# Taking engine orders from a scheduler with a re-tuned priority list, in an attention plus channel-mix kernel

## Chip, cores, metric

One core of one Trainium2 chip. The metric is device microseconds of one execution; lower is better. A kernel's time is the median of its runs. The spans in the traces are about 1.7 us shorter than the times (297.6 against 299.3 us for the profiled execution of the kernel before), because they run from the first to the last instruction.

## The reference

Batch 8, 8 heads, 576 positions, head dimension 64. Four heads attend to the last 32 positions, four to every fourth of the last 128. The attention output, laid out as x with 512 channels, goes through a channel mix:

```python
scores = where(mask, q @ k.T / 8, -1e9);  x = softmax(scores) @ v      # 8 batches
x_prev = x shifted by one position
xk = mu_k*x + (1-mu_k)*x_prev;   xr = mu_r*x + (1-mu_r)*x_prev
k  = relu(xk @ w_k);             v = (k*k) @ w_v                       # 512->1024->512
out = sigmoid(xr @ w_r) * v
```

## The kernel before

The kernel cuts the work into small steps and issues them from a list sorted by position. For attention, one batch needs T (transposes of q and k), six S (scores on TensorE, exp on ScalarE, mask multiply on VectorE), six P (value matmul on TensorE; reciprocal and multiply on VectorE) and three X (transposes of x; copies on ScalarE). S and P work on one block each, a stretch of 96 positions, so a batch has six blocks. A block also needs the 32 rows of v before it, its halo rows, which an on-chip shuffle copies into place. Then comes the interpolation, here called lerp: dx, md, xk, and md, xr on VectorE (dx is x minus x_prev; md is dx times murep, which holds mu - 1 repeated along the positions). The channel mix has nine tiles of 512 rows, each with eight K groups, four R groups and eight V groups of four matmuls.

```python
    def step_lerp_d(b):                        # dx: three VectorE operations
        ...
    def step_lerp_m(b, w):                     # md = dx * murep
        ...
    def plan_attn(b, base, cad, t0, tcad):
        ...
        for i in range(NB):
            at(base + cad * i, lambda i=i: step_S(b, i))
            at(base + cad * i + 2.2, lambda i=i: step_P(b, i))
            if i % 2 == 1:
                at(base + cad * i + 3.8, lambda i=i: step_X(b, i // 2))
        end = base + cad * 5 + 3.8
        at(end + 0.2, lambda: step_lerp_d(b))
        at(end + 0.3, lambda: step_lerp_m(b, 0))
        at(end + 0.4, lambda: step_lerp_a(b, 0))
        ...
    # ... (cut)
    with tc.manual_schedule(engines={ET.PE, ET.Activation, ET.DVE, ET.Pool}):
        for n in range(6):
            step_T(0, n, "act" if n % 2 == 0 else "dve")
        fix_v(0)                               # on-chip shuffle of v's halo rows
        make_murep(0); make_murep(1)           # 8 ScalarE copies
        ...
        for _, _, f in sorted(order, key=lambda t: t[:2]):
            f()
```

`manual_schedule` means that the named engines execute the program in the order in which it is written. Engines not named get an order from the compiler's scheduler, which takes the order of writing as a priority only. The order is fixed at compile time either way. In the traces an engine then waits at the next instruction in its order: in the run "The scheduler alone" below, VectorE stood 3.00 us at a scaling of wv, although the dx for the md behind it had been done for longer than that.

The softmax here doesn't subtract the row's maximum and nothing guards it: scores larger than these inputs give would overflow.

## Time and profile before

| | before |
|---|---|
| time, median (range), 3 runs | 298.81 us (297.08 to 299.91) |
| span of the profiled run | 297.6 us |
| ramp, to the first K matmul of tile 0 | 41.1 us |
| seven stages (tile 0 to 6, with attention of batches 1 to 7) | 217.2 us |
| tail (tiles 7 and 8, no attention left) | 39.3 us |

Two lines of the page. The first gives busy time, share of the span and instruction count of each engine; the second gives the clock that TensorE was granted in 40 equal slices of the span, in tenths of full speed.

```profile
PE 239.5 (80%) x2448; PEld 123.1 (41%) x2448; DVE 179.6 (60%) x349; ACT 158.5 (53%) x281; POOL 76.3 (26%) x123
...
PEclk9999999998699968999899979997999799999999
```

TensorE is the busiest engine, at 80%, and its clock dips in several slices (mean 0.954). The next view cuts the span at the first K matmul of each tile. Its columns are: the stretch, its length, busy us of TensorE, its weight loads, VectorE, ScalarE and GpSimd with instruction counts, granted clock, share of the DMA engines, GB/s. The first row is the ramp, then come stages 0 to 6.

```profile
0.00:41.09 41.09, 13.56 (x216) 10.67 (x217) 21.46 (x77) 16.30 (x26) 28.98 (x54) 1.00 1.67 147
41.09:75.18 34.09, 28.68 (x328) 14.39 (x328) 21.72 (x44) 19.80 (x35) 14.71 (x22) 0.96 1.46 153
75.18:107.47 32.29, 28.91 (x345) 15.45 (x345) 19.97 (x35) 20.67 (x37) 9.69 (x14) 0.92 0.66 86
107.47:143.26 35.79, 31.09 (x337) 15.69 (x338) 23.42 (x41) 19.93 (x36) 9.39 (x14) 0.88 0.72 96
143.26:174.30 31.04, 27.06 (x298) 13.63 (x297) 20.56 (x36) 18.21 (x33) 8.13 (x12) 0.94 0.70 96
174.30:205.08 30.78, 27.00 (x299) 13.70 (x298) 20.49 (x36) 18.21 (x33) 5.36 (x8) 0.94 0.56 90
205.08:235.80 30.72, 26.94 (x298) 13.63 (x298) 20.43 (x36) 18.22 (x33) 0.00 (x0) 0.94 0.13 35
235.80:258.28 22.48, 21.61 (x177) 10.36 (x177) 15.96 (x30) 13.09 (x24) 0.00 (x0) 0.99 0.13 36
```

Stages 3 to 5 (rows 143.26 to 235.80) take 30.7 to 31.0 us each with TensorE busy 27 us at a clock of 0.94. Who waits for whom on TensorE in the stages (us in total, times, longest; the 13.1 us include 5.3 us at the end of the ramp):

```profile
PE xo L236 <- DVE AT L221: 15.3, 4, 4.0
PE mm L310 <- DVE xk L298: 13.1, 4, 5.3
```

One such wait, in order of time. First VectorE, then TensorE; columns are start, duration, engine, line, operation, output and inputs, shapes, count, and in brackets the idle time before it and who ended it.

```profile
165.91 1.06 DVE L278 TENSOR_TENSOR dx<-xT 128x1728 f16<-128x1728 f16 x1 [2.63 <-ACT xT L268]
...
169.06 1.43 DVE L298 TENSOR_TENSOR xk<-md,xT 128x1024 f16<-128x1024 f16 x2
170.40 0.68 DVE L337 SCALAR_TENSOR_TENSOR ot<-sg,mm 128x512 f32<-128x512 f32 x1
171.00 0.55 DVE L221 TENSOR_TENSOR AT<-AT,mk 128x768 f16<-128x768 f16 x1
```

```profile
171.60 0.40 PE L236 MATMUL xo<-VAp,AT 128*128 128x65 f16 x4 [3.98 <-DVE AT L221]
171.82 0.41 PE L236 MATMUL xo<-VAd,AT 128*128 128x65 f16 x4
172.04 1.90 PE L333 MATMUL mm<-wv,k 128*128 128x512 f16 x4
```

VectorE does dx, md and xk of one batch in one row (165.91 to 170.4) and an output multiply (`ot`), and only then the mask multiply (`AT`) of the next batch, whose exp had ended at 166.65. TensorE stands idle 3.98 us for that mask multiply (`AT` in brackets). Its next four V matmuls take 1.90 us; the four before the hole took 1.03. After the hole the clock is half (0.50 from 171.6 to 174.8 by windows).

In the ramp, the chain of work that ended last reads (start, us, what):

```profile
14.28 5.31 ACT murep L127 x8
19.59 0.70 ACT AT L218
```

The eight murep copies sit in front of the first exp in ScalarE's queue.

### The profile page before, as it was taken

To read this page: it belongs to the slowest core of one execution; us is meant where nothing else is said; L and a number is where in the kernel's file an instruction comes from. 1 tells how busy PE (TensorE), PEld (TensorE's weight loads), DVE (VectorE), ACT (ScalarE), POOL (GpSimd) and SP (SyncE) were. 2 spreads that over 40 slices of the span, in tenths; PEclk is the share of its full clock that TensorE was granted. 3 is DMA by queue.
4 is the path that set the end of the run, shared out by engine and by line. 5 is a ranking of instruction groups with operands and counts; after the bars stand their busy time and mean duration, and the time that the engine had idled before them with its cause. 6 is when DMAs were issued, how large, how long until landed. Compare 5 with 4: busy or idle time off the path is not lost.

```text
span 297.6 us, 6026 instructions
## 1 busy us (share of the span) xinstructions
PE 239.5 (80%) x2448; PEld 123.1 (41%) x2448; DVE 179.6 (60%) x349; ACT 158.5 (53%) x281; POOL 76.3 (26%) x123
## 2 busy tenths in 40 slices
PE   0625349994889969994999599968998699899993
PEld 0513215442445634552455245533553344444441
DVE  4266392587377576558765676568656877772321
ACT  1484308853585737753586448643874285352530
POOL 8586575407210550037001800060000000000000
PEclk9999999998699968999899979997999799999999
DMA  8999999999391697039901990192011201113222
GB/s 87 146 166 198 134 169 172 138 127 162 44 154 39 96 134 138 0 82 122 200 3 37 137 202 29 37 126 79 2 37 37 70 3 37 35 72 87 56 63 78
DMA packets 57403, 27.80 MB, mean 93 GB/s; under 512 B 31776, under 2 KB 51744, under 8 KB 57376
## 3 DMA queue, kind: packets, MB, share of 16 engines
q0 software_dynamic: 49920, 16.78, 61.4%
q1 hardware_dynamic: 7456, 10.64, 11.9%
q8 instruction: 19, 0.31, 0.5%
q14 instruction: 8, 0.07, 0.1%
HBM read 33.56 MB, written 9.44 MB: 144 GB/s over the span
## 4 chain that ended last, share of the span: by engine, by line
PE 62%; DVE 19%; ACT 11%; issue 3%; DMA 3%; POOL 0%; POOLq 0%; DVEq 0%
PE mm L310 22%; PE mm L333 16%; PE mm L322 7%; PE xo L236 4%; DVE md L285 4%; DVE x L242 3%; PE tb L185 3%; PE ps L215 3%; PE tb L189 3%; ACT AT L218 3%; DVE dx L278 3%; DMA qk<-in_k_dram 3%; DVE xk L298 2%; DVE AT L221 2%; ACT murep L127 2%
## 5 line engine op out<-in xcount | busy, mean ns | idle before, releaser
L310 PE MATMUL mm<-xk,wk 128*128 128x512 f16 x288 | 77.5, 408 | 13.1 <-DVE xk L298 13.1
L333 PE MATMUL mm<-wv,k 128*128 128x512 f16 x288 | 75.8, 393 | 0.0
L315 ACT ACTIVATE kr<-mm 128x512 f16<-128x512 f32 x72 | 43.1, 601 | 38.1 <-PE mm L310 36.4
L218 ACT ACTIVATE AT<-ps 128x768 f16<-128x768 f32 x48 | 38.9, 810 | 34.2 <-PE ps L215 34.2
L77 POOL DMA_DIRECT2D VAp<-in_v_dram x32 | 23.1, 727 | 93.8 <-PE xo L236 92.4
L310 PEld LDWEIGHTS <-wk 128*128 128x128 f16 x288 | 26.2, 103 | 43.0 <-issue 15.5
L317 DVE TENSOR_TENSOR k<-kr 128x1024 f16<-128x1024 f16 x36 | 24.8, 691 | 31.7 <-ACT kr L315 31.7
L221 DVE TENSOR_TENSOR AT<-AT,mk 128x768 f16<-128x768 f16 x48 | 26.7, 557 | 25.1 <-ACT AT L218 25.0
L337 DVE SCALAR_TENSOR_TENSOR ot<-sg,mm 128x512 f32<-128x512 f32 x36 | 24.6, 684 | 23.7 <-PE mm L333 21.8
L322 PE MATMUL mm<-wr,xr 128*128 128x512 f16 x144 | 37.0, 379 | 0.0
L325 ACT ACTIVATE sg<-mm 128x512 f32<-128x512 f32 x36 | 21.6, 600 | 28.7 <-PE mm L322 28.6
L333 PEld LDWEIGHTS <-k 128*128 128x128 f16 x288 | 25.9, 100 | 26.5 <-issue 2.2
L242 DVE TENSOR_TENSOR x<-xo,rec 96x512 f16<-96x512 f32 x48 | 33.0, 687 | 1.6
L236 PE MATMUL xo<-VAp,AT 128*128 128x65 f16 x192 | 15.0, 204 | 21.7 <-DVE AT L221 15.3
L236 PEld LDWEIGHTS <-AT 128*128 128x128 f16 x384 | 18.0, 104 | 33.6 <-DVE AT L221 18.3
L168 ACT ACTIVATE QKp<-tb 128x384 f16<-128x384 f16 (+1 forms) x31 | 19.1, 645 | 11.1 <-PE tb L185 11.0
L168 ACT ACTIVATE QKd<-tb 128x768 f16<-128x768 f16 (+1 forms) x29 | 18.4, 659 | 8.7 <-PE tb L189 8.7
L85 POOL DMA_DIRECT2D VAd<-in_v_dram x32 | 19.9, 630 | 11.1 <-DMA qk<-in_k_dram 5.8
L185 PE MATMUL tb<-ident,qk 48*64 48x48 f16 (+1 forms) x512 | 15.1, 207 | 9.3 <-DMA qk<-in_q_dram 7.2
L285 DVE TENSOR_TENSOR md<-dx,murep 128x2304 f16<-128x2304 f16 x16 | 21.7, 1355 | 0.3
L215 PE MATMUL ps<-QKp 64*128 64x96 f16 x192 | 13.5, 221 | 7.1 <-ACT AT L218 7.0
L185 PEld LDWEIGHTS <-qk 48*64 48x64 f16 (+1 forms) x512 | 12.1, 117 | 16.7 <-DMA qk<-in_q_dram 7.2
(50 smaller groups left out, 245.6 us busy)
## 6 DMA issues: line engine op xcount, KB each, us to landing
qk<-in_q_dram POOLq DMA_DIRECT2D x8, 384.0 KB, 6.3
qk<-in_k_dram POOLq DMA_DIRECT2D x8, 384.0 KB, 8.5
VAp<-in_v_dram POOLq DMA_DIRECT2D x32, 72.0 KB, 4.8
out_dram<-ot SPq DMA_DIRECT2D x8, 256.0 KB, 2.5
out_dram<-ot SPq DMA_DIRECT2D x8, 224.0 KB, 2.5
qk<-in_q_dram POOLq DMA_DIRECT2D x8, 192.0 KB, 9.3
qk<-in_k_dram POOLq DMA_DIRECT2D x8, 192.0 KB, 9.1
VAd<-in_v_dram POOLq DMA_DIRECT2D x16, 96.0 KB, 4.3
```

The costliest lines, as they stand in the source:

```text
L168: nc.scalar.activation(out=out, in_=in_, func=AF.Copy)
L185: nc.tensor.transpose(out=tv[par * D:(par + 1) * D, wi, sl, :], in_=t[:nj, w, 2 * hp + par, r * D:(r + 1) * D], identity=ident[:nj, :nj])
L218: nc.scalar.activation(out=at[:, :, :, 0:QB], in_=ps[:, :, 0:4 * QB].rearrange("p a (s x) -> p a s x", s=4), func=AF.Exp, scale=0.125)
L221: nc.vector.tensor_tensor(out=at[:, :, :, 0:QB], in0=at[:, :, :, 0:QB], in1=MK[combos[i]], op=ALU.mult)
L236: nc.tensor.matmul(out=xo[:, pr, par * (D + 1):(par + 1) * (D + 1)], lhsT=w, rhs=va[:, o + par:o + par + D + 1], start=True, stop=True)
L242: nc.vector.tensor_tensor(out=x16[:QB].rearrange("p a g d -> p g a d"), in0=xo[:QB, :, 1:VW].rearrange("p g (a d) -> p g a d", a=2), in1=r ...
L285: nc.vector.tensor_tensor(out=md, in0=xT_of[(b, "dx")], in1=murep[:, w], op=ALU.mult)
L310: nc.tensor.matmul(out=pk, lhsT=wk[:, c, f * 128:(f + 1) * 128], rhs=xk_t[tt][:, c], start=(c == 0), stop=(c == 3))
L315: nc.scalar.activation(out=kr[:, f % 2], in_=pk, func=AF.Relu, scale=8.0)
L317: nc.vector.tensor_tensor(out=k2_of[tt][:, f - 1:f + 1], in0=kr, in1=kr, op=ALU.mult)
L322: nc.tensor.matmul(out=pr, lhsT=xr_t[tt][:, c, ts * 128:(ts + 1) * 128], rhs=wr[:, c], start=(c == 0), stop=(c == 3))
L333: nc.tensor.matmul(out=pv, lhsT=k2_of[tt][:, f, ts * 128:(ts + 1) * 128], rhs=wv[:, f], start=(f == 0), stop=(f == 7))
```

## The change

Its intent is to let the scheduler order TensorE, ScalarE and VectorE, with a list tuned for that: attention starts earlier against the tiles, the value step lags more, the interpolation is issued in six pieces. In the ramp, murep goes from ScalarE to VectorE, the masks need 8 copies in place of 32, the mask construction on GpSimd goes ahead of the loads of v, and the transposes of x come one step later. The core of the diff:

```diff
-    load_batch(0)
+    for jc in range(2):
+        load_qk(0, jc)                  # load_v(0) now follows the mask work
...
-            nc.scalar.activation(out=murep[:, w, c], in_=ones, func=AF.Copy, scale=mu[:, w, c:c + 1])
+            nc.vector.tensor_scalar(out=murep[:, w, c], in0=ones, scalar1=mu[:, w, c:c + 1], scalar2=None, op0=ALU.mult)
...
-    def plan_attn(b, base, cad, t0, tcad):
+    def plan_attn(b, base, cad, t0, tcad, lag=2.2):
...
-            at(base + cad * i + 2.2, lambda i=i: step_P(b, i))
+            at(base + cad * i + lag, lambda i=i: step_P(b, i))
...
-        at(end + 0.2, lambda: step_lerp_d(b))
-        at(end + 0.3, lambda: step_lerp_m(b, 0))
-        at(end + 0.4, lambda: step_lerp_a(b, 0))
-        at(end + 2.5, lambda: step_lerp_m(b, 1))
-        at(end + 4.5, lambda: step_lerp_a(b, 1))
+        at(end + 0.2, lambda: step_lerp_d(b, 0))
+        at(end + 0.8, lambda: step_lerp_d(b, 1))
+        at(end + 1.3, lambda: step_lerp_m(b, 0))
+        at(end + 2.0, lambda: step_lerp_a(b, 0))
+        at(max(end + 4.0, G * b + 2.5), lambda: step_lerp_m(b, 1))
+        at(max(end + 5.5, G * b + 4.5), lambda: step_lerp_a(b, 1))
...
-    plan_attn(1, 8.0, 1.5, 4.2, 0.7)    # likewise for batches 2 and 3
+    plan_attn(1, 6.3, 1.4, 3.0, 0.6)
-        base = G * (b - 1) - 3.5
-        plan_attn(b, base, 3.0, base - 16.5, 3.0)
+        base = G * (b - 1) - 6
+        plan_attn(b, base, 3.0, base - 16.5, 3.0, 3.0)
...
-    with tc.manual_schedule(engines={ET.PE, ET.Activation, ET.DVE, ET.Pool}):
+    with tc.manual_schedule(engines={ET.Pool}):
```

More of the change, by code (lines that the diff above doesn't have):

```diff
@@ L123 @@
     murep = const.tile([128, 2, 4, S], FP16, name="murep")
-    def make_murep(w):
+    for w in range(2):
         for c in range(4):
-            nc.scalar.activation(out=murep[:, w, c], in_=ones, func=AF.Copy, scale=mu[:, w, c:c + 1])
+            nc.vector.tensor_scalar(out=murep[:, w, c], in0=ones, scalar1=mu[:, w, c:c + 1], scalar2=None, op0=ALU.mult)
     m01 = const.tile([128, 3, QB], FP16, name="m01")
@@ L142, with make_masks @@
     MK = {}
-    for combo in ((START, START), (FULL, START), (FULL, MID), (FULL, FULL)):
-        t = const.tile([128, 2, 4, QB], FP16, name=f"mk{combo[0]}{combo[1]}")
-        for par in range(2):
-            for sl in range(4):
-                nc.vector.tensor_copy(out=t[:, par, sl], in_=m01[:, combo[sl // 2]])
-        MK[combo] = t
+    def make_masks(combos):
+        for combo in combos:
+            t = const.tile([128, 2, 4, QB], FP16, name=f"mk{combo[0]}{combo[1]}")
+            for g in range(2):
+                nc.vector.tensor_copy(out=t[:, :, 2 * g:2 * g + 2],
+                                      in_=m01[:, combo[g]].unsqueeze(1).unsqueeze(1).to_broadcast([128, 2, 2, QB]))
+            MK[combo] = t
+    load_v(0)
     combos = [(START, START), (FULL, START), (FULL, MID), (FULL, MID), (FULL, FULL), (FULL, FULL)]
@@ L273, with step_lerp_d @@
     xk_t, xr_t = {}, {}
-    def step_lerp_d(b):
+    def step_lerp_d(b, part):
         xT = xT_of[b]
-        dx = lerp_p.tile([128, 4, S], FP16, name="dx")
-        nc.vector.tensor_tensor(out=dx[:, :, J:S], in0=xT[:, :, J:S], in1=xT[:, :, 0:S - J], op=ALU.subtract)
-        nc.vector.tensor_tensor(out=dx[:, :, 1:J], in0=xT[:, :, 1:J], in1=xT[:, :, 3 * J:S - 1], op=ALU.subtract)
-        nc.vector.tensor_copy(out=dx[:, :, 0:1], in_=xT[:, :, 0:1])
-        xT_of[(b, "dx")] = dx
+        if part == 0:
+            xT_of[(b, "dx")] = lerp_p.tile([128, 4, S], FP16, name="dx")
+        dx = xT_of[(b, "dx")]
+        if part == 0:
+            nc.vector.tensor_tensor(out=dx[:, :, J:S], in0=xT[:, :, J:S], in1=xT[:, :, 0:S - J], op=ALU.subtract)
+        else:
+            nc.vector.tensor_tensor(out=dx[:, :, 1:J], in0=xT[:, :, 1:J], in1=xT[:, :, 3 * J:S - 1], op=ALU.subtract)
+            nc.vector.tensor_copy(out=dx[:, :, 0:1], in_=xT[:, :, 0:1])
     def step_lerp_m(b, w):
@@ L365, in plan_attn @@
             at(t0 + tcad * 5 + 0.1, lambda: [load_qk(b + 2, jc) for jc in range(2)])
-            at(base + cad * 5 + 2.3, lambda: load_v(b + 2))
+            at(base + cad * 5 + lag + 0.1, lambda: load_v(b + 2))
         at(base - 2, lambda: fix_v(b))
@@ L369, in plan_attn @@
             at(base + cad * i, lambda i=i: step_S(b, i))
-            at(base + cad * i + 2.2, lambda i=i: step_P(b, i))
+            at(base + cad * i + lag, lambda i=i: step_P(b, i))
             if i % 2 == 1:
-                at(base + cad * i + 3.8, lambda i=i: step_X(b, i // 2))
-        end = base + cad * 5 + 3.8
-        at(end + 0.2, lambda: step_lerp_d(b))
-        at(end + 0.3, lambda: step_lerp_m(b, 0))
-        at(end + 0.4, lambda: step_lerp_a(b, 0))
-        at(end + 2.5, lambda: step_lerp_m(b, 1))
-        at(end + 4.5, lambda: step_lerp_a(b, 1))
+                at(base + cad * i + lag + 2.4, lambda i=i: step_X(b, i // 2))
+        end = base + cad * 5 + lag + 2.4
+        at(end + 0.2, lambda: step_lerp_d(b, 0))
[4 more added lines that the diff above has]
+        at(max(end + 5.5, G * b + 4.5), lambda: step_lerp_a(b, 1))
     G = 20
@@ L389 @@
     at(-2, lambda: load_batch(2))
-    plan_attn(1, 8.0, 1.5, 4.2, 0.7)
-    plan_attn(2, 25.0, 1.7, 18.5, 1.0)
-    plan_attn(3, 41.5, 2.0, 33.5, 1.3)
+    plan_attn(1, 6.3, 1.4, 3.0, 0.6)
+    plan_attn(2, 24.5, 1.7, 18.5, 0.9)
+    plan_attn(3, 41.0, 2.0, 33.5, 1.3)
     for b in range(4, B):
-        base = G * (b - 1) - 3.5
-        plan_attn(b, base, 3.0, base - 16.5, 3.0)
-    with tc.manual_schedule(engines={ET.PE, ET.Activation, ET.DVE, ET.Pool}):
+        base = G * (b - 1) - 6
+        plan_attn(b, base, 3.0, base - 16.5, 3.0, 3.0)
+    with tc.manual_schedule(engines={ET.Pool}):
         for n in range(6):
             step_T(0, n, "act" if n % 2 == 0 else "dve")
+        make_masks([(START, START)])
         fix_v(0)
-        make_murep(0)
-        make_murep(1)
         step_S(0, 0)
         for i in range(NB):
+            if i == 0:
+                make_masks([(FULL, START)])
             if i + 1 < NB:
                 step_S(0, i + 1)
+            if i == 0:
+                make_masks([(FULL, MID), (FULL, FULL)])
+            if i in (2, 4):
+                step_X(0, i // 2 - 1)
             step_P(0, i)
-            if i % 2 == 1:
-                step_X(0, i // 2)
-        step_lerp_d(0)
+        step_X(0, 2)
+        step_lerp_d(0, 0)
+        step_lerp_d(0, 1)
         for w in range(2):
```

## The prediction

> **What bounds the kernel now.** By the page TensorE is busy 239.5 of 297.6 us, VectorE 179.6. In the chain that ended last, the first channel-mix matmul (L310) of tiles 0 to 7 starts at 41.1, 75.2, 107.5, 143.3, 174.3, 205.1, 235.8 and 258.3 us; then matmuls to the end. So: ramp 41 us, seven stages 217 us, tail 39 us.
>
> In the stages TensorE stands idle 25.7 us (217 minus the busy times by windows). The waits list names two causes: the attention-value matmuls wait for the mask multiply on VectorE (15.3 us, 4 times), each tile's first matmul for xk (about 7 us). The timeline at 165.9 to 171.6 shows how: VectorE does dx, md and xk of one batch in a row, then an output multiply, and only then the next batch's mask multiply; TensorE idles 4.0 us. After each such hole the windows show a granted clock of 0.5 for about 3 us, a further 1.7 us. The Trainium skill, "TensorE: Matmul & The Clock Gate", section "What's actually happening", gives an idle window of about 3.4 us as what drops the clock to half; the trace agrees (holes of 4 to 5 us, then 0.50). One stage takes 30.7 us, of which about 25.0 is matmul work at full clock.
>
> **The change.**
> - Ramp: eight ScalarE copies of murep (5.31 us on the chain, 14.28 to 19.59) become eight VectorE operations (estimate 1.7 us, as the same form on wv takes) in idle time. The 32 mask copies (3.33 us) become 8. The first exp moves from 19.5 to about 14 us. But block 1 waits for the shuffle of v, landing at 21.7 us, block 2 for the second, at 23.7 (they ran at 23.2 and 25.7). These landings should stay. From 23.8 us on, four blocks of about 1.6 us, transposes, copies and the lerp chain of 4.3 us put L310 at about 36 (35.5 to 37.5) instead of 41.1: minus 5 us.
> - Stages: the instruction orders show the lerp chain split, with output multiplies, reciprocals and mask multiplies between its parts, and more matmuls between the last x transposes and the next tile. With the trace's durations a late stage has about 6.4 us of matmul work against a chain of about 6.5, so the hole shrinks from 4 us to 0.5 to 1.5 and the clock mostly stays up. The first three boundaries have only 3 to 5 us of work there: holes of 2 to 3 us remain.
>
> **Sum.** Ramp minus 5; stage 0 34.1 to about 30; stage 1 32.3 to 29.5; stage 2 35.8 to 31.5; stages 3 to 5 30.8 to 27.5 each; last minus 1. About 27 us less: **272 us, 8 in 10 between 260 and 286**. Faster by over 2%: 0.93; within 2%: 0.04; slower: 0.03.
>
> **What would show it.** ScalarE's first exp at 14 us; first L310 at 36; tile starts 26 to 28.5 us apart from tile 3 on; waits of value matmuls for the mask multiply down from 15 us to under 5; mean clock up from 0.954 to 0.97 or more; tail 39 us.
>
> **What would make it wrong.** The scheduler's fixed orders suit its own durations: an engine that waits in order for something late (scaling of wv behind its load near 43 us, the early copy of dx's first column) could open new holes. Shuffles landing later would eat the ramp's gain. If holes close entirely, 258.

## The result

The changed kernel takes 270.48 us (269.85 to 271.23, 4 runs), against 299.36 us for the kernel before in the same rounds. The ratio is 0.9048, with a 95% interval of 0.8992 to 0.9104. Ratios here are the mean time of one kernel's fast runs over that of the other's fast runs of the same rounds, so they are not quite the ratio of the medians quoted.

The same lines of the page after:

```profile
PE 234.4 (87%) x2448; PEld 126.4 (47%) x2448; DVE 177.2 (66%) x333; ACT 153.7 (57%) x273; POOL 76.3 (28%) x123
...
PEclk9999999999799995999999999999999999999999
```

And the same cut at the first K matmul of each tile, columns as before:

```profile
0.00:36.53 36.53, 14.19 (x217) 11.08 (x217) 23.13 (x61) 11.07 (x18) 25.62 (x48) 1.00 1.77 150
36.53:68.51 31.98, 29.34 (x333) 14.92 (x332) 22.14 (x44) 19.67 (x35) 18.15 (x28) 1.00 1.61 171
68.51:101.40 32.89, 30.55 (x385) 16.67 (x386) 20.69 (x37) 23.23 (x40) 9.70 (x14) 0.93 0.75 102
101.40:131.44 30.04, 29.23 (x329) 15.46 (x328) 20.18 (x38) 19.99 (x36) 9.37 (x14) 0.90 1.01 127
131.44:156.04 24.60, 24.52 (x279) 13.65 (x278) 18.43 (x34) 17.39 (x32) 8.14 (x12) 1.00 0.51 72
156.04:181.71 25.67, 25.37 (x297) 14.30 (x296) 19.48 (x36) 18.20 (x33) 5.36 (x8) 1.00 0.81 117
181.71:207.48 25.77, 24.98 (x282) 13.85 (x281) 19.57 (x36) 17.49 (x32) 0.00 (x0) 1.00 0.18 52
207.48:229.53 22.05, 21.51 (x177) 10.89 (x177) 18.49 (x34) 12.29 (x23) 0.00 (x0) 1.00 0.19 55
```

| stretch | before | after | difference | predicted after |
|---|---|---|---|---|
| ramp | 41.1 | 36.5 | -4.6 | 36 |
| stage 0 | 34.1 | 32.0 | -2.1 | 30 |
| stage 1 | 32.3 | 32.9 | +0.6 | 29.5 |
| stage 2 | 35.8 | 30.0 | -5.8 | 31.5 |
| stage 3 | 31.0 | 24.6 | -6.4 | 27.5 |
| stage 4 | 30.8 | 25.7 | -5.1 | 27.5 |
| stage 5 | 30.7 | 25.8 | -4.9 | 27.5 |
| stage 6 | 22.5 | 22.1 | -0.4 | 21.5 |
| tail | 39.3 | 39.4 | 0 | 39 |

The differences add up to the 28.7 us between the spans. Stage 1 got no shorter, though stage 0 ends earlier: it now holds 385 matmul instructions instead of 345 (TensorE's count in the windows), while the later stages hold fewer. The earlier positions bring attention work forward into it.

The 1.00 in the row of stage 0 can't be taken at its word: the first 16 K matmuls there took 6.50 us, and 3.61 in the run "The parts together", where matmuls fill the hole ahead of them. The half clock at the start of tile 0 is missing from the record.

The waits of TensorE in the stages, after (of the 7.1 us, 5.1 are at the end of the ramp):

```profile
PE xo L239 <- DVE AT L224: 2.8, 4, 1.4
PE mm L316 <- DVE xk L304: 7.1, 4, 5.1
```

The same place of a late stage on VectorE:

```profile
177.00 0.56 DVE L224 TENSOR_TENSOR AT<-AT,mk 128x768 f16<-128x768 f16 x1 [1.45 <-ACT AT L221]
177.77 1.06 DVE L284 TENSOR_TENSOR dx<-xT 128x1728 f16<-128x1728 f16 x1 [0.21 <-ACT xT L271]
178.75 0.45 DVE L286 TENSOR_TENSOR dx<-xT 128x572 f16<-128x572 f16 x1
179.12 0.68 DVE L343 SCALAR_TENSOR_TENSOR ot<-sg,mm 128x512 f32<-128x512 f32 x1
179.71 1.35 DVE L291 TENSOR_TENSOR md<-dx,murep 128x2304 f16<-128x2304 f16 x1
180.98 0.20 DVE L242 RECIPROCAL rec<-xo 96x8 f32<-96x8 f32 x1
181.10 1.43 DVE L304 TENSOR_TENSOR xk<-md,xT 128x768 f16<-128x768 f16 x2
```

The mask multiply of the next batch (177.00) now comes ahead of dx, and an output multiply stands between dx and md. Meanwhile TensorE had work: K of the next tile starts at 181.71 without a hole, straight after the V matmuls.

```profile
179.87 1.90 PE L339 MATMUL mm<-wv,k 128*128 128x512 f16 x8
181.71 1.02 PE L316 MATMUL mm<-xk,wk 128*128 128x512 f16 x4
```

The whole chain from dx to the end of xk takes 4.8 us here, and no longer holds up the start of the tile.

In the ramp, the chain that ended last now reads:

```profile
14.60 6.87 DMA VAp<-VAp
21.51 0.64 PE xo L239 x8
```

The second block waits for the landing of the shuffle of v (`VAp<-VAp`), as the prediction had it for 21.7 us. In the kernel before, this block ran at 23.17. So 1.7 us of the ramp's 4.6 are gained up to there; the other 2.9 lie in the steps after it, which take 15.0 us to the end of the ramp instead of 17.9.

### The profile page after: what moved, and what is told of

Read it like the earlier page. It is cut to its first block, busy times and chain, and to the rows that moved or that the text cites. A ratio compares the mean times of both kernels' runs of the same rounds, so it can differ in the third digit from the quotient of the medians.

```text
span 268.9 us, 5996 instructions
## 1 busy us (share of the span) xinstructions
PE 234.4 (87%) x2448; PEld 126.4 (47%) x2448; DVE 177.2 (66%) x333; ACT 153.7 (57%) x273; POOL 76.3 (28%) x123
## 3 DMA queue, kind: packets, MB, share of 16 engines
q1 hardware_dynamic: 7456, 10.64, 13.4%
## 4 chain that ended last, share of the span: by engine, by line
PE 69%; DVE 13%; ACT 7%; DMA 5%; issue 4%; POOL 0%; POOLq 0%; DVEq 0%
PE mm L316 24%; PE mm L339 16%; PE mm L328 10%; PE xo L239 5%; DVE md L291 4%; PE tb L192 4%; PE ps L218 3%; PE tb L188 3%; DMA VAp<-VAp 3%; DMA qk<-in_k_dram 2%; DVE xk L304 2%; DVE ot L343 2%; ACT AT L221 1%; DVE x L245 1%; PE tb L259 1%
## 5 line engine op out<-in xcount | busy, mean ns | idle before, releaser
L316 PE MATMUL mm<-xk,wk 128*128 128x512 f16 x288 | 75.2, 405 | 7.7 <-DVE xk L304 7.6
L339 PE MATMUL mm<-wv,k 128*128 128x512 f16 x288 | 71.2, 380 | 0.0
L321 ACT ACTIVATE kr<-mm 128x512 f16<-128x512 f32 x72 | 43.7, 607 | 39.7 <-PE mm L316 39.1
L316 PEld LDWEIGHTS <-wk 128*128 128x128 f16 x288 | 27.2, 103 | 39.7 <-issue 7.8
L323 DVE TENSOR_TENSOR k<-kr 128x1024 f16<-128x1024 f16 x36 | 24.7, 687 | 21.9 <-ACT kr L321 21.8
L339 PEld LDWEIGHTS <-k 128*128 128x128 f16 x288 | 25.3, 97 | 26.0
L343 DVE SCALAR_TENSOR_TENSOR ot<-sg,mm 128x512 f32<-128x512 f32 x36 | 24.6, 684 | 18.8 <-PE mm L339 17.4
L224 DVE TENSOR_TENSOR AT<-AT,mk 128x768 f16<-128x768 f16 x48 | 26.2, 548 | 12.0 <-ACT AT L221 11.8
L242 DVE RECIPROCAL rec<-xo 96x8 f32<-96x8 f32 x48 | 9.6, 201 | 21.8 <-PE xo L239 21.6
L188 PE MATMUL tb<-ident,qk 48*64 48x48 f16 (+1 forms) x512 | 15.8, 208 | 8.0 <-DMA qk<-in_q_dram 6.7
L328 PEld LDWEIGHTS <-xr 128*128 128x128 f16 x144 | 13.4, 98 | 14.9
```

Source lines behind the costliest of these rows:

```text
L224: nc.vector.tensor_tensor(out=at[:, :, :, 0:QB], in0=at[:, :, :, 0:QB], in1=MK[combos[i]], op=ALU.mult)
L316: nc.tensor.matmul(out=pk, lhsT=wk[:, c, f * 128:(f + 1) * 128], rhs=xk_t[tt][:, c], start=(c == 0), stop=(c == 3))
L321: nc.scalar.activation(out=kr[:, f % 2], in_=pk, func=AF.Relu, scale=8.0)
L323: nc.vector.tensor_tensor(out=k2_of[tt][:, f - 1:f + 1], in0=kr, in1=kr, op=ALU.mult)
L328: nc.tensor.matmul(out=pr, lhsT=xr_t[tt][:, c, ts * 128:(ts + 1) * 128], rhs=wr[:, c], start=(c == 0), stop=(c == 3))
L339: nc.tensor.matmul(out=pv, lhsT=k2_of[tt][:, f, ts * 128:(ts + 1) * 128], rhs=wv[:, f], start=(f == 0), stop=(f == 7))
```

## The experiments

The question was which part did it: the scheduler, the list, or the ramp edits; whether the half clock really costs time; and what bounds the ramp. The table has the ratio of each run to the kernel before in its own rounds.

| run | median us | ratio | ramp ends at |
|---|---|---|---|
| before | 299.0 to 299.4 | 1 | 41.1 |
| new ramp alone, program order | 296.38 | 0.9921 | 37.0 |
| scheduler alone, old list and ramp | 276.30 | 0.9251 | 35.7 |
| new list and ramp, program order | 276.18 | 0.9254 | 36.1 |
| new list, scheduler, old ramp | 269.95 | 0.9040 | 36.6 |
| the change (all of it) | 270.48 | 0.9048 | 36.5 |

### The new ramp alone

```diff
# the kernel before, with the ramp of the changed kernel;
# list positions, unsplit lerp and manual_schedule of all engines kept
```

> The kernel before with the whole new ramp (masks and loads reordered, murep as vector operations, transposes of x one step later), but with the old priority list and all engines in program order. Theory A (ramp and stages are two separate gains that add): the first channel-mix matmul starts at 37 us instead of 41, the stages stay as they were (tile starts 30.7 us apart late, 4 us holes), total about 295 us. Rival (most of the gain comes from the ramp, because the DMA queues run earlier and everything shifts): under 285 us.

Measured: 296.38 us (295.94 to 297.07), ratio 0.9921 (0.9865 to 0.9977). The ramp ends at 36.97 us, 4.1 us earlier. The stages keep their holes: waits for the mask multiply are again 15.3 us in 4. Stage 0 takes 35.1 us instead of 34.1, so 1 us is given back. The ramp edits alone are worth about 2.7 us of the span, under 1% of the time; theory A stands here. The second block ran at 22.37, and the steps after it took 14.6 us to the end of the ramp, 3.3 less than in the kernel before: the gain lies there more than in the first exp (15.32 here).

### The scheduler alone

```diff
-    with tc.manual_schedule(engines={ET.PE, ET.Activation, ET.DVE, ET.Pool}):
+    with tc.manual_schedule(engines={ET.Pool}):      # on the kernel before
```

> The kernel before with one change: only the GpSimd order stays in program order, so the scheduler orders TensorE, VectorE and ScalarE from the OLD priority list. Theory A (the scheduler itself closes the holes): about 278 us, waits of the value matmuls for the mask multiply under 6 us. Rival B (the new positions in the list close them, the scheduler alone does not): over 293 us with the 4 us holes still there.

Measured: 276.30 us (274.99 to 278.06), ratio 0.9251. No wait of a value matmul for the mask multiply is left. The VectorE order at the same place of a late stage shows why:

```profile
184.68 0.45 DVE L279 TENSOR_TENSOR dx<-xT 128x572 f16<-128x572 f16 x1
185.04 0.55 DVE L221 TENSOR_TENSOR AT<-AT,mk 128x768 f16<-128x768 f16 x1
185.51 1.35 DVE L285 TENSOR_TENSOR md<-dx,murep 128x2304 f16<-128x2304 f16 x1
```

The scheduler put the mask multiply (185.04) between dx and md. Stages 3 to 5 take 26.2 to 26.4 us; holes of 0.6 to 0.9 us that wait for xk remain at the starts of tiles 4 to 6. The ramp ends at 35.66 us with the old ramp code: the scheduler moved murep to ScalarE's idle time by itself. But stage 0 takes 36.5 us, 4.5 more than in the changed kernel. VectorE shows what it met there:

```profile
38.81 0.39 DVE L161 TENSOR_SCALAR wv<-wv 128x512 f16<-128x512 f16 x1 [3.00 <-DMA wv<-in_moe_w_v_dram]
```

It stood 3.00 us waiting for the load of wv in the middle of tile 0.

### The new list in program order, with the new ramp

```diff
-    with tc.manual_schedule(engines={ET.Pool}):      # on the changed kernel
+    with tc.manual_schedule(engines={ET.PE, ET.Activation, ET.DVE, ET.Pool}):
```

> The changed kernel with all engines forced back to program order, so the NEW priority list is executed literally. Theory A (the scheduler does it): about 285 us, most of the holes at tile starts come back, only the ramp's gain and a part of the stages remain. Rival B (the list positions do it): 269 to 274 us, like the changed kernel.

Measured: 276.18 us (275.69 to 278.06), ratio 0.9254. This lies between what the theory (285) and the rival (269 to 274) expected, so neither holds. In program order the new list also has the mask multiply ahead of dx, in fact directly ahead:

```profile
180.46 0.56 DVE L224 TENSOR_TENSOR AT<-AT,mk 128x768 f16<-128x768 f16 x1 [1.45 <-ACT AT L221]
181.22 1.06 DVE L284 TENSOR_TENSOR dx<-xT 128x1728 f16<-128x1728 f16 x1 [0.21 <-ACT xT L271]
```

Waits for the mask multiply fall from 15.3 to 3.3 us, and stages 3 to 5 take 26.3 to 26.8 us. Ahead of tiles 1 to 3, waits for xk of 2.0 to 3.6 us remain. Scheduler and list are therefore two ways to much the same gain: each without the other brings about 7.5%, both together 9.5%. This run also has the new ramp, which was worth 0.8% alone; the new list in program order with the old ramp was not run. No run moved the mask multiply alone either: in both, the order of other steps changed too.

### The old ramp under the new list and the scheduler

```diff
# the changed kernel with load order, murep on ScalarE, 32 mask copies
# and the order of the first batch's steps as before
```

> The changed kernel with the old ramp put back (loads of v ahead of the mask work on GpSimd, 32 mask copies, murep on ScalarE), new list and scheduler kept. The compiled order already shows that the scheduler moves murep ahead of the first exp by itself. Theory A: then murep costs nothing, the masks end near 19 us, the shuffle of v (21.5 us) remains what the second block waits for, so the first channel-mix matmul moves only from 36.5 to about 37.5 and the total is about 272 us. Rival (the ramp edits themselves carry their 5 us): about 275.5 us.

Measured: 269.95 us (269.41 to 270.81), ratio 0.9040, the same as the change. The ramp ends at 36.58 us. The mask copies now end at about 19.5 us, but the second block waits until about 21.9 us anyway. Once the scheduler orders the engines, the ramp edits are worth nothing measurable. This went further than expected (272).

### murep early, still on ScalarE

```diff
     with tc.manual_schedule(engines={ET.PE, ET.Activation, ET.DVE, ET.Pool}):    # the kernel before
+        make_murep(0)
+        make_murep(1)
         for n in range(6):
             step_T(0, n, "act" if n % 2 == 0 else "dve")
         fix_v(0)
-        make_murep(0)
-        make_murep(1)
```

> The kernel before with one move: the eight ScalarE copies of murep are issued before the first transposes instead of after them; still on ScalarE, everything else as before. Theory A (their place in the ScalarE queue held up the first exp, not the engine): first exp at about 14 us, but the 32 mask copies then end at about 19 us on VectorE, so the first mask multiply gains only about 1 us and the first channel-mix matmul starts at 39.5 to 40.5 us; total 297.5. Rival (moving murep away was worth its 5.3 us): first channel-mix matmul at 36 us, total about 294.

Measured: 298.23 us (295.72 to 298.71), ratio 0.9942 (0.9885 to 0.9998). The first exp starts at 14.33 us instead of 19.49, the ramp ends at 39.53. The next thing in the row is the 32 mask copies, on VectorE:

```profile
15.69 3.33 DVE L147 COPY mk<-m 128x96 f16<-128x96 f16 x32 [1.07 <-POOL m L135]
```

They hold the first mask multiply until 18.94, and the second block then waits for the shuffle until 21.72. Taking 5.3 us off the chain in one place moved its end by 1.6 us, as theory A had it. From the second block to the end of the ramp it still takes 17.8 us; with the new ramp in program order it took 14.6 to 14.7, with the scheduler and the old ramp 14.5 to 14.7. So the rest of the ramp's gain comes from the order of the steps after that block, the transposes of x one step later among them; which of them it is was not tested.

### murep on ScalarE in the changed kernel

```diff
-            nc.vector.tensor_scalar(out=murep[:, w, c], in0=ones, scalar1=mu[:, w, c:c + 1], scalar2=None, op0=ALU.mult)
+            nc.scalar.activation(out=murep[:, w, c], in_=ones, func=AF.Copy, scale=mu[:, w, c:c + 1])
```

> The changed kernel with murep back on ScalarE, all else kept. The compiled order puts the eight copies ahead of the first exp. Theory A: no change, 270 to 271 us, first channel-mix matmul at 36.5 us. Rival (VectorE for ScalarE is part of the gain): 273 us or more.

Measured: 269.90 us (268.13 to 270.67), ratio 0.9001, ramp to 36.47 us. Which engine does murep plays no part that shows here; its place in the queue does (the run before this one: 1.6 us of the ramp).

### The interpolation at its old positions

```diff
-        at(end + 0.8, lambda: step_lerp_d(b, 1))
-        at(end + 1.3, lambda: step_lerp_m(b, 0))
-        at(end + 2.0, lambda: step_lerp_a(b, 0))
-        at(max(end + 4.0, G * b + 2.5), lambda: step_lerp_m(b, 1))
-        at(max(end + 5.5, G * b + 4.5), lambda: step_lerp_a(b, 1))
+        at(end + 0.2, lambda: step_lerp_d(b, 1))
+        at(end + 0.3, lambda: step_lerp_m(b, 0))
+        at(end + 0.4, lambda: step_lerp_a(b, 0))
+        at(end + 2.5, lambda: step_lerp_m(b, 1))
+        at(end + 4.5, lambda: step_lerp_a(b, 1))
```

> The changed kernel with the six interpolation steps put back to the old positions in the list (subtraction, first product and first sum directly after each other, second product and sum where they were). If the split of the interpolation is what lets mask multiplies and output multiplies through, the waits of value matmuls for the mask multiply go from 2.8 us to over 8 us and the total to 276 to 282 us. Rival (the scheduler's interleaving is enough): 269 to 272.5 us.

Measured: 269.10 us (267.05 to 270.82), ratio 0.9001, waits for the mask multiply 2.2 us. The six positions of the interpolation are not what closes the holes: with the old list too, the scheduler put a ready mask multiply between its parts (185.04 above). The 1.4 us by which the median is lower is not a gain that is shown: the intervals overlap, and in the profiled run the first 16 matmuls of tile 0 took 5.03 us where they took 6.50 in the changed kernel.

### Halo rows loaded straight

```diff
+    # float32 halo rows of v, batch 0, on SyncE's queue at the start, then ScalarE casts them into place
+        nc.sync.dma_start(out=hp[:, :, h], in_=v[0, h].rearrange("(i p) d -> p i d", p=QB)[QB - PAD:QB, 0:NB - 1])
+        nc.scalar.activation(out=VAp[0][0:PAD, 1:NB, o:o + D], in_=hp[:, :, h], func=AF.Copy)
+    # ... likewise for the other four heads
-        fix_v(0)
```

> The changed kernel, but for the first batch the 32 halo rows of v are loaded straight from HBM as float32 on the idle queue of SyncE at the start and cast by ScalarE, so the second block of attention does not wait for the on-chip shuffle (21.5 us). If that landing bounds the ramp as the prediction says: second block at about 17.5 us, first channel-mix matmul at 32 to 33.5 us, total about 267 us. Rival (the ramp is bound by the serial chain exp, mask, value matmul, normalisation, or by the loads): first channel-mix matmul later than 35.5 us and total over 269.5 us.

Measured: 267.80 us (265.91 to 268.94), ratio 0.8934. The ramp ends at 34.65 us, outside both expectations. The wait for the shuffle is gone: the second block runs at 20.11 us instead of 21.51. But the transposes of k, at 8.80 us in the changed kernel, came at 10.73, after a wait for the load of k; the first exp starts at 14.32 us instead of 12.40. The Trainium skill, "DMA: Bandwidth & Descriptors", section "Issuing engines are not separate DMA queues", says that transfers started by different engines interleave on the same 16 DMA engines, so the added loads may have held up k. The runs don't show it: without added loads these transposes came anywhere from 8.80 to 10.98 us (10.98 in the new ramp in program order). So the shuffle did bound the ramp, and behind it lies the chain that begins with the arrival of k. Of the 4.6 us between the spans of the two profiled runs the ramp is 1.9; much of the rest is less half clock (the first 16 matmuls of tile 0 took 5.31 us, not 6.50; stage 2 has clock 0.94, not 0.90).

### Keeping TensorE busy in the holes of the kernel before

```diff
+    def warm(b, n):                                   # result read by nobody
+        pd = p_mm.tile([128, 512], FP32, name="mm")
+        for i in range(n):
+            nc.tensor.matmul(out=pd, lhsT=ident, rhs=xT_of[b][:, i % 4, 0:512], start=True, stop=True)
+    at(19.99, lambda: warm(1, 12)); at(39.99, lambda: warm(2, 9)); at(58.65, lambda: warm(3, 12))
+    at(78.65, lambda: warm(4, 12)); at(98.65, lambda: warm(5, 12)); at(118.65, lambda: warm(6, 12))
     # and warm(0, 10) after step_lerp_d(0)
```

> The kernel before, in its own order, with matmuls whose result nobody reads put into the seven holes (10, 12 and 9 ahead of tiles 0, 1 and 2, 12 in each of the four later holes); they read x of the batch just transposed and take about 2.6 us of a 4 us hole. If the half clock after a hole costs the 1.7 us per hole that the prediction put on it: clock 0.98 or more, tile starts 29 us apart from tile 3 on instead of 30.7, total 286 to 290 us though 79 matmuls were added. Rival (the cold clock is a reading without a cost, only the idle time counts): 298 us or more, tile starts still 30.7 us apart.

Measured: 286.33 us (285.76 to 286.35), ratio 0.9570 (0.9527 to 0.9613). With 79 matmuls more, the kernel is 4.3% faster. The mean clock is 0.998 instead of 0.954, and the late stages take 29.2 to 29.4 us instead of 30.7 to 31.0. The first 20 matmuls of tile 0, before and in this run:

```profile
41.09 6.52 PE L310 MATMUL mm<-xk,wk 128*128 128x512 f16 x20 [5.25 <-DVE xk L298]
```

```profile
40.54 4.77 PE L310 MATMUL mm<-xk,wk 128*128 128x512 f16 x20 [0.16 <-DVE xk L298]
```

The half clock after a hole has a cost of its own, here 1.5 us per late hole and 1.75 us in tile 0, beside the idle time.

### The same in the changed kernel

```diff
+        if b in (1, 2):
+            at(end + 2.05, lambda: warm(b, {1: 8, 2: 5}[b]))
     # and warm(0, 9) after the first batch's lerp_d
```

> The changed kernel with unread matmuls in its three remaining holes: 9 ahead of tile 0, 8 ahead of tile 1, 5 ahead of tile 2. If the cold clock is what is left there: tile 0's first 16 matmuls take about 3.7 us instead of 6.5, the half clock after tiles 1 and 2 goes, total 263 to 266 us. Rival (these stages are bound by the chain of the attention, not by TensorE's clock): 269 us or more.

Measured: 264.39 us (262.18 to 266.54), ratio 0.8822. The profiled run is the slowest of the six. In it stage 0 falls from 32.0 to 29.1 us (the first 16 matmuls from 6.50 to 3.61), stage 1 from 32.9 to 30.9; the profile of the next run, a fast one, has the same 29.1 and 30.9. Stage 2 kept its cold start, that is half clock (0.89 over the stage). The other five runs have clocks from 0.991 to 1.000 and are mostly the faster the higher it is (265.12 us twice at 0.991, 262.18 to 263.65 at 0.996 to 1.000). It seems that the last hole keeps the clock up in some executions and not in others; these five have no trace, and why was not settled.

### The parts together

```diff
# the changed kernel with the old lerp positions, the straight halo loads and the unread matmuls
```

> Halo rows loaded straight, interpolation steps at the old positions, and the unread matmuls, on top of the changed kernel: a version meant to beat both. If the parts add (2 us of halo, 1 us of positions, 4 to 6 us of clock): 260 to 263 us. If the unread matmuls do not help: 266 to 268 us.

Measured: 261.67 us (260.93 to 263.69), ratio 0.8757 (0.8722 to 0.8792), result correct. This beats both kernels. The ratio is 0.029 below that of the change, where the three parts alone were 0.011, 0.005 and 0.023 below it: they add in large part, not fully.

### The old list under the scheduler, without scaling wv

```diff
-    at(10.5, scale_wv)        # result wrong by the factor 128, on purpose
```

> The old list under the scheduler (as in the run old list, scheduler: 276.3 us), with the scaling of wv by 1/128 left out; the result is wrong on purpose by that factor, all other work is the same. In that run VectorE stood 3.0 us waiting for wv's load in the middle of tile 0, and the stage of tile 0 took 36.5 us against 32.0 in the changed kernel. If that early place of the scaling is what the new list avoided: stage 0 falls to 32 to 33.5 us and the total to 271 to 273 us. Rival (the new attention positions are what shortens stage 0): stage 0 stays over 35 us, total over 275 us.

Measured: 274.48 us (273.55 to 276.06), ratio 0.9218, against 0.9251 with the scaling, in other rounds. Stage 0 falls from 36.5 to 33.4 us, as expected of the scaling. The total fell less than expected, into the gap between the two expectations; the intervals of the two ratios overlap. So 3.1 of the 4.5 us that the old list lost in stage 0 came from the early scaling, visible in the stage and not resolved in the total. The edit takes out the wait for the load (3.00 us) and also the scaling itself (VectorE is busy 1.6 us less in the stage); the two were not separated. Against the changed kernel, stages 3 to 6 of this run are 0.5 to 1.8 us longer each, stage 0 1.5 us longer, while the ramp and stages 1 and 2 are 1.0, 0.6 and 1.1 us shorter. What remains of the changed kernel's advantage is the sum of these; which position is worth what stays open.

## Why the prediction was right

- **Total.** Predicted 272 us (260 to 286), measured 270.48. The size came out close partly because two errors cancelled: stages 0 and 1 were predicted 5.4 us too short together, stages 2 to 5 were predicted 8 us too long.
- **Ramp.** First exp predicted at 14, measured 12.40, mostly because k landed sooner (its transposes at 8.80 us, 10.14 before). Over the runs they came anywhere from 8.80 to 10.98, so that is at least in part luck; it bought nothing, since the shuffle came last. Predicted end 36, measured 36.5; block 1, the second one, predicted at 21.7, measured 21.51, waiting for the shuffle. The mechanism held. The attribution did not: the prediction put the 5 us down to the murep and mask edits, but the scheduler gets the same from the old ramp (35.7 us), and taking the edits out of the changed kernel costs nothing (269.95 us).
- **murep.** The step "estimate 1.7 us, as the same form on wv takes" was mis-sized: the eight operations took 3.96 us. wv is scaled by a constant, murep by a value per partition, so it was not quite the same form; and GpSimd built masks and issued loads at the same time, while single murep operations took anything from 0.36 to 0.70 us. What made them slower was not tested. It cost nothing, because VectorE had nothing else to do until 9.7 us.
- **Late stages.** Predicted 27.5 us with holes of 0.5 to 1.5; measured 24.6 to 25.8 with holes of at most 0.43 inside these stages. The cause named, lerp in one row ahead of the mask multiply, was right as far as the runs go: two different ways of moving the mask multiply ahead (scheduler, list) take the 4 us hole away. The split of the lerp, which the prediction also named, is not needed.
- **First boundaries.** Holes of 2 to 3 us were predicted; measured 0.91 + 1.50 ahead of tile 1, 0.90 + 1.43 ahead of tile 2, and 0.65 + 0.16 ahead of tile 3. The term that was mis-sized most is stage 1, 29.5 predicted and 32.9 measured: the prediction did not count that the new positions bring 40 more matmul instructions into it, and dropped the half clock after its hole (clock 0.93). The half clock is about 1.7 us of the miss: with the same 385 instructions at clock 0.98, in the run with the old ramp, the stage took 31.2. Stage 0 was predicted at 30 and took 32.0. There the prediction does not mention the half clock after the ramp's 5.1 us hole: with that hole filled, in "The parts together", the first 16 matmuls took 2.9 us less and the stage 29.1.
- **How much the half clock varies.** With the hole ahead of tile 0 unchanged at 5.1 us, its first 16 matmuls took 6.50 us in the change, 6.14 with murep on ScalarE, 5.31 with the halo loads and 5.03 with the old interpolation positions. So a difference of 1 to 2 us between two such runs need not come from their edits.
- **Waits and clock.** Waits for the mask multiply 2.8 us (predicted under 5), clock 0.979 (0.97 or more), tail 39.4 (39).

## What to carry to other kernels

When an in-order engine serves two pipelines, look at which instruction stands in front of the one that the bottleneck waits for; here two means that moved it ahead were worth about the same (7.5% each, one of them with the new ramp), and together 9.5%, far from 15. An edit that takes 5 us off a chain may move its end by 1.6, because the next thing in the row was only slightly behind. A hole on TensorE can cost its idle time and a stretch at half clock, so filling a hole that cannot be closed with unread matmuls can pay.

## What the Trainium skill lacked or had wrong

- "TensorE: Matmul & The Clock Gate", section "What's actually happening", puts the drop to half clock after an idle window of about 3.4 us. Here shorter holes dropped it too: in the kernel before, one of 2.38 us ahead of tile 2 (0.50 for the 3 us after it). So did a partly filled one, and the same kind of hole did not in another run. The changed kernel with 1.21 us of work in 3.4 us, and the run with the new list in program order with 0.98 us in 3.8 us, by windows:

```profile
98.00:101.40 3.40, 1.21 (x21) 0.83 (x21) 3.40 (x6) 1.52 (x2) 1.05 (x2) 0.86 1.22 127
101.40:106.80 5.40, 5.40 (x43) 2.48 (x42) 3.74 (x6) 2.35 (x5) 1.24 (x2) 0.50 1.20 191
```

```profile
66.00:69.80 3.80, 0.98 (x20) 0.49 (x18) 3.77 (x7) 1.15 (x2) 1.50 (x3) 1.00 1.49 184
69.80:75.00 5.20, 5.20 (x76) 2.89 (x77) 2.09 (x3) 4.05 (x8) 1.54 (x2) 1.00 0.63 109
```

  The first was followed by 5.4 us at 0.50, longer than the page's 3.4 us of warming up; the second by none. The page's remark that the window runs freely fits this, but no run here shows where the window lay.
- The same page describes the trace's clock events and warns of them, but does not say that the record can be missing at the start: the granted clock reads 1.00 for the whole ramp and from there to 60 us in both kernels, while the first 16 matmuls of tile 0 in the changed kernel took 6.50 us, and 3.61 us in the two runs that put unread matmuls ahead of them (one of these profiles fast, one slow).
- "DMA: Bandwidth & Descriptors", section "Issuing engines are not separate DMA queues", says that transfers interleave, but gives no figure for what loads on a second queue cost those already running. The runs don't settle it: with 0.3 MB of halo rows added (worked out from the shapes, in float32) the transposes of k came at 10.73 and 10.64 us; in the four other runs with the new ramp under the scheduler at 8.80 to 9.84, but in two runs without added loads at 10.89 and 10.98.
